# First MoE's first product as plain 512-column products beside the attention, instead of seven products for eight

## The chip, the cores and the metric

The kernel runs on one core of one Trainium2 chip. The metric is the device time of one execution in microseconds (us); less is better. Of several executions the median is given. A profile is one execution taken by the hardware profiler; its span runs from the first to the last instruction.

## The reference

Three stages follow each other: causal attention with a decay, then two MoE layers (each one a dense pair of products, without routing). Cut to what is computed:

```python
# q, k, v: (4, 8, 576, 64), f: (4, 8, 576)
cum = cumsum(log(clip(f, 1e-4, 1)))                      # per batch and head
scores = q @ k.T / sqrt(64) + cum[:, None] - cum[None, :]
attn = softmax(where(causal, scores, -1e9)) @ v
x = attn, heads side by side                             # (2304, 512)
h = x @ w_in;  g = h * clip(h + 3, 0, 6) / 6;  x = g @ w_out      # first MoE, w_in (512, 2048)
h = x @ w_in2; g = softplus(h);                out = g @ w_out2   # second MoE
```

The weight matrices arrive as 64-bit floats, and the kernel turns their words into 32-bit floats itself.

## The kernel before, in words

**The work.** The attention goes by 16 pairs of heads (4 batches of 4 pairs). For a pair: q and k are loaded in runs of 32 elements and transposed by VectorE (`qk_job`, L563); the scores are products of 64 rows (`s_job`, L609), VectorE takes the row minimum with the decay added (L631) and ScalarE the exponential (L640); TensorE transposes the result (`t_job`, L703; copied out at L725), multiplies it with v (`pv_job`, L750), and VectorE scales by the inverse of the row sums, which went through DRAM to be spread over the partitions (`inv_job`, L674, L758). The pair's x goes to DRAM (L763). The decays come from DRAM too (L568), for the first pair from TensorE (`first_decays`, L583).

**The four MoE products** are made seven for eight (the Strassen-Winograd scheme: seven products of sums of quarter matrices instead of eight of the quarters). Each product of 32-bit numbers is three matmuls of rounded parts: high x high, high x low, low x high. So every factor is split by ScalarE (high part, a copy with rounding) and VectorE or GpSimd (low part, a difference).

- First product of the first MoE: `step_a(0, t, p)`, four blocks t of 576 tokens (a batch each), eight pairs p of 128-column tiles of w_in. A step is 7 products x 2 x 3 = 42 matmuls of 288 columns (L1064). They are summed by ScalarE copies (L1080) and VectorE additions (L1083), then come Relu (L1108) and a min-and-multiply (L1109), and a store of g (L1116).
- Its x factors, `factors_x(0, t)`: loads from DRAM (L998), four differences (L1022) and seven splits (L1017, L1018). For t < 3 all blocks use the one buffer MX, and the differences lie in HY[0], the tile into which the products are summed; `freed(hkeys(0), fours)` and back order the two uses.
- Its weight factors, `weights(0, 0, p)`: two loads of 512 KB into two staging tiles (L858), conversion (L878, L880, L881), four sums (L925), splits into U[p] (L954, L957).
- Second product: `step_c`, blocks of 512 and 256 tokens, 42 or 21 matmuls of 256 columns a step (L1220), g loaded from DRAM and factored (`factors_g`, L1151, L1162, L1173, L1177); its weights are converted earlier and stored in DRAM (`convert`, L888), loaded again (L913), and factored by `weights(0, 1, p)`.
- The second MoE follows in the same way: `step_a(1, t, p)` (L1064), `step_b` (L1275).

**The order.** All operations are given to a planner (`Work.order`) with a cost, a due time `at` and what they read and write. It goes through them in its own model of time and writes one fixed order for each engine; transfers nearly all go through SP's queue in that order. On the chip an engine waits for whatever its next instruction needs. The due times come from the table `PLAN`: T0, D1, D2, D3 place the blocks of the first product beside the attention, b0 and the gaps place the ends of the batches, u0 to u3 and c1 to c3 the weights; capA and capH limit the PSUM banks that attention and first product hold (eight in all).

**The tiles.** In the attention's time the space on the right holds two more sets of score tiles (pc, pd) and a second xs. They are closed after pair 5 (NZ = 6) to make room for U[6] and U[7]; from pair 6 on there are two sets and one xs. After the attention `open_m2` opens XO, HY[1], XT, GR and two more staging tiles; the last x block of the first product goes to XO, and so waits for it.

Of the kernel before, what the change touches and what calls it, by code (L numbers as in the profile page):

```python
# [20 lines left out]
S_JOBS = [[[(4, 0, 288)], [(4, 288, 576)]], [[(3, 0, 448)]], [[(2, 0, 320)], [(1, 0, 192), (0, 0, 64)]]]  # L21
# [30 lines left out]
    NZ=6,  # L52
    pc=4087.38,
    pp=2327.32,
    pv=84.33,
    bend=[1.23, 1.22, 0.82, 0.85],
    b0=45.58,
    T0=63.44,
    D1=71.18,
    D2=126.72,  # L60
    D3=92.29,
    gap=35.47,
    gap2=34.18,
    gap3=57.23,
    cA=2.46,
    SA=5.95,
    SC=5.87,
    SB=2.2,
    iva=10.96,
    nwarm=18,  # L70
    sp=-2.13,
    evb=-2.3,
    u0=-9.63,
    u1=6.1,
    u2=12.94,
    u3=4.01,
    fx=-4.74,
    ul=20.0,
    c1=18.83,
    c2=53.66,  # L80
    c3=7.91,
    cvw=16.39,
    ldw=121.83,
    xa=36.77,
    xs=3.98,
    ga=3.94,
    tsp=-32.98,
    xat=0.0,
    xl=6.7,
    rel=96.88,  # L90
    wfrom=22.68,
    lv0=9.67,
    lq1=14.03,
    decst=4.47,
    capH=3,
    capA=8,
    eps=0,
    slp=45.39,
    slv=33.59,
    lat=1.39,  # L100
# [200 lines left out]
def attention_two_moe_kernel(  # L301
# [24 lines left out]
    NA, NG = S, 2 * P  # L326
    CB = [(0, TB), (TB, NG)] + [(TB + NG + i * TB, TB) for i in range((NT - TB - NG) // TB)]
# [18 lines left out]
    g1_dram = [dp.tile([NF, P, S], F32, name=f"g1_dram{b}") for b in range(B)]  # L346
# [33 lines left out]

    T0 = K["T0"]

    BLK = [T0, T0 + K["D1"], T0 + K["D1"] + K["D2"], T0 + K["D1"] + K["D2"] + K["D3"]]
    MC = BLK[3] + K["SA"] * NPR
    M2_0 = MC + K["SC"] * NPR * NT / TB
    MB = M2_0 + K["SA"] * NPR * (NT // NA)

    def a_at(m, t, p, x=0.0):

        if m:  # L390
            return M2_0 + K["SA"] * (t * NPR + p + x)
        if t == 3:
            return BLK[3] + K["SA"] * (p + x)
        return BLK[t] + (BLK[t + 1] - BLK[t]) * ((p + x) / NPR) ** (K["cA"] if t == 0 else 1.0)
# [21 lines left out]

    IV = ap.tile([P, P], F32, name="bar")
# [7 lines left out]
    MX = mp.tile([P, 7 * XW], F32R, name="MX")  # L425
# [11 lines left out]

    NZ = K["NZ"]
    FW = NPR - 2
    T = {}  # L440
    side = ctx.enter_context(ExitStack())
# [22 lines left out]
    def open_early():  # L464
        a = side.enter_context(tc.tile_pool(name="apw", bufs=1, side="right"))
        T["xs"].append(a.tile([P, S], F32, name="xs2"))
        T["P"] = [PS, PS2]
        for z in "cd":
            t = a.tile([P, sum(PW)], F32, name="p" + z)
            T["P"].append([t[:, sum(PW[:i]):sum(PW[:i + 1])] for i in range(len(PW))])  # L470

    def set_of(pn, i):

        return (2 * pn + i) % 4 if pn < NZ else i

    U = []

    def open_late_w():
        side.close()
        a = ctx.enter_context(tc.tile_pool(name="lw", bufs=1, side="right"))  # L480
        for p in range(FW, NPR):
            U.append(a.tile([P, UW], F32R, name=f"U{p}"))

    st = [mp.tile([P, NC * P, 2], U32, name=f"st{i}") for i in range(2)]
    for p in range(FW):
        U.append(wp.tile([P, UW], F32R, name=f"U{p}"))

    op(("sp", 1.0, open_early), w=["early"], at=-9)
    openers = {"w": op(("sp", 1.0, open_late_w), w=["latew"], name="latew")}
# [4 lines left out]
    def fill_by(name, n, tiles, value, w, at=0.0, r=("early",), one=False):  # L494
        ways = [("pool", 0.9 * n + 60, lambda: nc.gpsimd.memset(tiles(), value)), ("dve", 1.04 * n + 8, lambda: nc.vector.memset(tiles(), value))]
        op(ways[:1] if one else ways, w=w, r=r, at=at, name=name)
# [4 lines left out]
    for i in range(2):  # L501
        fill_by("fv", P, lambda i=i: T["vr"][i][KCUT[-1][1]:, 4].rearrange("p h d -> p (h d)"), 0.0, [("vz", i)], one=True)
# [796 lines left out]
    for d in last_att:  # L1299
        for m in d.early:  # L1300
            openers[m].deps[d] = 1
# [111 lines left out]
```

## Time and profile before

| what | us |
|---|---|
| median of 3 runs | 994.32 (993.56 to 995.84) |
| profiled execution | 999.6 |
| its span | 997.8 |

In the profile's rows, L12 is line 12 of the kernel before. PE is TensorE's matmuls, PEld its weight loads, DVE VectorE, ACT ScalarE, POOL GpSimd, SP the engine that issues the transfers (SPq: its queue's instructions). A matmul's busy time is longer than its share of a steady run, since matmuls overlap; pace is therefore read from a stretch's length over its count. PEclk is the granted TensorE clock as a share of 2.4 GHz. `<-` in square brackets names what ended an idle time.

### The profile page before, as it was taken

What the parts mean: (1) busy time and instruction counts of PE and PEld (TensorE: products, weight loads), DVE (VectorE), ACT (ScalarE), POOL (GpSimd) and SP (SyncE); (2) the same over time, 40 slices, a digit from 0 to 9 for tenths busy, and PEclk for the clock granted to TensorE, in tenths of its full rate; (3) what the DMA queues carried; (4) which work ended last, traced back from release to release, by engine and by line L of the source; (5) the groups of instructions that cost most, each with busy time, mean ns of one, the idle gap of its engine ahead of it and who ended that gap; (6) DMA issues with size and microseconds to landing.
All of it is one profiled execution on the core that took longest, in us unless ns stands there. A gap on an engine that the chain in (4) does not pass through costs nothing.

```text
span 997.8 us, 19909 instructions
## 1 busy us (share of the span) xinstructions
PE 936.3 (94%) x7156; PEld 869.1 (87%) x7156; DVE 770.2 (77%) x1671; ACT 598.9 (60%) x1202; POOL 120.1 (12%) x250
## 2 busy tenths in 40 slices
PE   9888698988999898989999999999999989999997
PEld 5665587866896787989999999999999989999997
DVE  4676787967676767999879789988564877888885
ACT  3877777886777755864345355777566753333342
POOL 2232111220112002200010110300010100010000
PEclk6999899997999899998999999999999999999999
DMA  6778948799978686764553454699823643435342
GB/s 92 176 171 208 216 138 232 206 231 234 261 255 263 208 298 233 243 191 148 163 160 106 149 156 131 211 336 367 292 98 127 207 143 108 128 125 165 115 129 79
DMA packets 210467, 187.07 MB, mean 187 GB/s; under 512 B 108800, under 2 KB 161152, under 8 KB 210368
## 3 DMA queue, kind: packets, MB, share of 16 engines
q1 hardware_dynamic: 207744, 185.43, 62.4%
q8 instruction: 56, 0.92, 0.4%
q10 hardware_dynamic: 2624, 0.37, 0.3%
q14 instruction: 43, 0.35, 0.1%
HBM read 121.12 MB, written 64.63 MB: 186 GB/s over the span
## 4 chain that ended last, share of the span: by engine, by line
PE 66%; DVE 13%; DMA 10%; ACT 4%; issue 3%; SPq 2%; POOL 0%; ACTq 0%; DVEq 0%; POOLq 0%
PE bank L1064 31%; PE bank L1275 18%; PE bank L1220 10%; DVE MX L1177 2%; PE bank L609 2%; DMA st<-in_moe_w_in_dram 2%; DVE U L957 2%; PE bank L750 2%; PE bank L703 2%; SPq L527 1%; DMA st<-in_moe_w_out_dram 1%; DMA kr<-in_k_dram 1%; DVE st L925 1%; DVE HY L1162 1%; DMA ivb<-inv_dram 1%
## 5 line engine op out<-in xcount | busy, mean ns | idle before, releaser
L1064 PE MATMUL bank<-MX,U 128*128 128x288 f32 x1680 | 248.1, 304 | 17.1 <-ACT HY L1080 9.1
L1064 PEld LDWEIGHTS bank<-MX,U 128*128 128x128 f32 x1680 | 232.3, 192 | 27.2 <-ACT HY L1080 14.4
L1275 PE MATMUL bank<-U,XO 128*128 128x256 f32 x1512 | 181.4, 282 | 2.8 <-ACT XO L1173 2.0
L1275 PEld LDWEIGHTS bank<-U,XO 128*128 128x128 f32 x1512 | 180.7, 190 | 3.4 <-ACT XO L1173 2.2
L1220 PE MATMUL bank<-MX,U 128*128 128x256 f32 x1344 | 162.4, 282 | 5.0 <-DVE MX L1177 3.9
L1220 PEld LDWEIGHTS bank<-MX,U 128*128 128x128 f32 x1344 | 160.1, 190 | 6.6 <-DVE MX L1177 4.8
L1080 ACT ACTIVATE HY<-bank 128x288 f32<-128x288 f32 x256 | 101.2, 406 | 63.1 <-PE bank L1064 48.4
L1064 PE MATMUL bank<-XO,U 128*128 128x288 f32 x1008 | 137.6, 297 | 1.3 <-DVE HY L1083 1.1
L1064 PEld LDWEIGHTS bank<-XO,U 128*128 128x128 f32 x1008 | 135.2, 188 | 2.2 <-DVE HY L1083 1.6
L1083 DVE TENSOR_TENSOR HY<-HY,bank 128x288 f32<-128x288 f32 x192 | 84.8, 449 | 57.6 <-PE bank L1064 53.7
L624 POOL TENSOR_SCALAR_AFFINE_SELECT w<-w 128x128 f32<-128x128 f32 (+1 forms) x160 | 57.6, 368 | 240.9 <-DVE stats L631 173.8
L957 DVE TENSOR_TENSOR U<-st,U 128x768 fp32r<-128x768 f32 (+1 forms) x63 | 70.9, 1133 | 7.1 <-ACT U L954 6.9
L609 PE MATMUL bank<-KT,QT 64*128 64x288 f32 (+4 forms) x384 | 67.8, 446 | 8.7 <-ACT pt L725 6.6
L954 ACT ACTIVATE U<-st 128x1024 fp32r<-128x1024 f32 (+1 forms) x64 | 59.9, 949 | 12.1 <-DVE st L925 8.2
L725 ACT ACTIVATE pt<-bank 128x448 f32<-128x448 f32 (+2 forms) x127 | 57.6, 499 | 11.2 <-PE bank L703 10.0
L1108 ACT ACTIVATE HY<-HY,half 128x576 f32<-128x576 f32 x64 | 49.3, 774 | 21.5 <-DVE HY L1083 19.5
L609 PEld LDWEIGHTS bank<-KT,QT 64*128 64x128 f32 x384 | 39.0, 200 | 25.2 <-ACT pt L725 10.0
L1109 DVE SCALAR_TENSOR_TENSOR HY<-HY 128x576 f32<-128x576 f32 x64 | 49.8, 780 | 12.8 <-ACT HY L1108 12.6
L750 PEld LDWEIGHTS bank<-pt,vr 128*64 128x64 f32 x512 | 35.1, 142 | 23.6 <-DVE stats L631 5.5
L881 DVE SCALAR_TENSOR_TENSOR st<-st 128x512 uint32<-128x512 uint32 x64 | 44.3, 692 | 14.3 <-ACT st L878 10.6
L1173 ACT ACTIVATE MX<-GR 128x768 fp32r<-128x768 f32 x36 | 30.4, 844 | 40.6 <-PE bank L1220 33.6
L750 PE MATMUL bank<-pt,vr 128*64 128x256 f32 (+3 forms) x512 | 52.7, 352 | 1.3 <-DVE stats L631 0.9
(145 smaller groups left out, 1276.2 us busy)
## 6 DMA issues: line engine op xcount, KB each, us to landing
GR<-g_dram SPq DMA_DIRECT2D x52, 512.0 KB
g_dram<-HY SPq DMA_DIRECT2D x64, 288.0 KB
g_dram<-HY SPq DMA_DIRECT2D x32, 576.0 KB
st<-in_moe_w_in_dram SPq DMA_DIRECT2D x32, 512.0 KB
st<-in_moe_w_out_dram SPq DMA_DIRECT2D x32, 512.0 KB
wf_dram<-st SPq DMA_DIRECT2D x48, 256.0 KB
st<-wf_dram SPq DMA_DIRECT2D x48, 256.0 KB
w<-dec_dram SPq DMA_DIRECT2D x30, 288.0 KB
```

The source lines that it names most:

```text
L609: nc.tensor.matmul(bank[bks[h, y].i][:, o:o + c - a], T["Q"][z][h * D:h * D + D, q0:q0 + P], T["K"][z][h * D:h * D + D, a:c], start=lead, ...
L624: nc.gpsimd.affine_select(out=blk, in_=blk, compare_op=ALU.is_ge, fill=-1e9 / scale, base=0, pattern=[[-1, r]], channel_multiplier=1)
L725: e.activation(out=place(i, j, a, c), in_=src(), func=ACTF.Copy)
L750: nc.tensor.matmul(acc[i * D:i * D + D, s + k0 - a:c - a], T["vr"][z][:, j, i], place(i, j, s, c - k0), start=(n < 2), stop=(n >= len(todo ...
L954: op(("act", act(n * h, False), lambda src=src, to=to: nc.scalar.activation(out=to(0), in_=src(), func=ACTF.Copy)), r=rd, w=w, at=at, name ...
L957: e.tensor_tensor(to(1), src(), to(0).bitcast(F32), op=ALU.subtract)
L1064: nc.tensor.matmul(bank[bks[b].i][:, 0:HA], wa[u][:, c], xa[v][:, c], start=(nm in ("P1", "P2", "P5") and c == 0 and y == 0), stop=(c == 1 ...
L1080: op(("act", act(HA, True) + 30, lambda: nc.scalar.activation(out=to(q), in_=bp(), func=ACTF.Copy)), r=new, banks=[ba], w=[("H", i, q)], a ...
L1083: op(("dve", dve(HA), lambda: nc.vector.tensor_tensor(to(q), to(q), bp(), op=ALU.add)), r=new, banks=[ba], w=[("H", i, q)], at=at, name="a ...
L1109: op2(("dve", dve(n), lambda h=h: nc.vector.scalar_tensor_tensor(out=h(1), in0=h(1), scalar=1.0, in1=h(0), op0=ALU.min, op1=ALU.mult)), r= ...
L1220: nc.tensor.matmul(bank[bks[b].i][:, o * 256:(o + 1) * 256], *ops, start=(p == 0 and o == 0 and y == 0), stop=(p == NPR - 1 and y == 2), s ...
L1275: nc.tensor.matmul(bank[bks[b].i][:, o * 256:(o + 1) * 256], ga[u], wa[v], start=(p == 0 and o == 0 and y == 0), stop=(p == NPR - 1 and y ...
```

## The change

**The first product is plain.** Tokens go in blocks of 512 (four, and one of 256) and tiles `ft` of 128 columns of w_in, 16 of them. A step has 4 x 3 matmuls of 512 (or 256) columns into one bank, and no sums; Relu and the min-and-multiply read the bank:

```diff
+    GB = [(i * TB, min(TB, NT - i * TB)) for i in range(-(-NT // TB))]
...
+    def step_g(t, ft):
...
+        bk = Bank(att_banks, "h")
+        for c in range(NC):
+            def go(c=c):
...
+                for y, (w, x) in enumerate(((wh, xh), (wh, xl), (wl, xh))):
+                    nc.tensor.matmul(bank[bk.i][:, 0:n], w, x, start=(c == 0 and y == 0), stop=(c == NC - 1 and y == 2))
...
+        g = HY[0][:, i * TB:i * TB + n]
...
+        ev = at - K["evb"]
+        op(("act", act(n, True, 1) + 10, lambda: nc.scalar.activation(out=g, in_=bank[bk.i][:, 0:n], func=ACTF.Relu, scale=1.0 / 6.0, bias=half)), r=["half"], banks=[bk], w=[("g", i)], at=ev, name="relu")
+        op(("dve", dve(n), lambda: nc.vector.scalar_tensor_tensor(out=g, in0=g, scalar=1.0, in1=bank[bk.i][:, 0:n], op0=ALU.min, op1=ALU.mult)), banks=[bk], w=[("g", i)], at=ev, name="g")
+        dma(lambda: nc.sync.dma_start(out=g1_dram[ft, :, a0:a0 + n], in_=g), 4 * P * n, r=[("g", i)], w=[("gd", 0, t, ft)], at=at - 1, name="storeg")
```

`i` goes round four output buffers in HY[0]. g lies in one DRAM tensor over all tokens, so that the second product's loads of g are no longer cut at batch ends.

**Weights and x are only split.** `weights_g(ft)` loads and converts one tile and makes its high and low part. `load_g(t)` loads x by the four 128-row parts and splits each in place; block t lies in half t % 2 of MX. Block 0 is split from the attention's own tile:

```diff
+        if b == 0:
+            xh, xl = (XG(0)[z][:, hp] for z in range(2))
+            op(("act", act(TB, False), lambda: nc.scalar.activation(out=xh, in_=X()[:, 0:TB], func=ACTF.Copy)), r=xk, w=[("X", 0, hp)], at=at - K["xat"], name="xh")
+            op2(either(TB, lambda e: e.tensor_tensor(xl, X()[:, 0:TB], xh.bitcast(F32), op=ALU.subtract)), r=xk, w=[("X", 0, hp)], at=at - K["xat"], name="xl")
```

**Tiles.** The first product's weight parts W1 lie in the tiles U[3] to U[7]: ft 0 and 1 in U[3], seven parts each in the others. U[0] is free from the start, U[1] and U[2] are opened after the attention. Blocks 0 to 2 go beside the attention; the last two go together, tile by tile, and each unit of the second product's weights is made when the parts in its tile are used up:

```diff
+    for t in (LG, LG + 1):
+        load_g(t, BLK[3] - K["xa"] + 0.5 * (t - LG))
+    made = 3
+    for ft in range(NF):
+        for t in (LG, LG + 1):
+            step_g(t, ft)
+        while made < NPR and all(k[1] <= ft for k in on_tile[made]):
+            freed(on_tile[made], [("unit", made, 0), ("unit", made, 1)])
+            weights(0, 1, made, c_at(0, made) - K["u1"], made % 2 * 2, False)
+            made += 1
```

Unit 0 is made before, units 1 and 2 after `open_m2`.

**Attention.** `early`, `latew` and NZ go; all 16 pairs have four score sets and two xs. The scores are five jobs of at most one bank a head, and the first pair's heads go together too:

```diff
-S_JOBS = [[[(4, 0, 288)], [(4, 288, 576)]], [[(3, 0, 448)]], [[(2, 0, 320)], [(1, 0, 192), (0, 0, 64)]]]
+S_JOBS = [[[(4, 0, 288)]], [[(4, 288, 576)]], [[(3, 0, 448)]], [[(2, 0, 320)]], [[(1, 0, 192), (0, 0, 64)]]]
...
-        heads = (0, 1) if pn else (i,)
+        heads = (0, 1)
```

The first pair's decay matmuls use all 128 rows, for which GpSimd fills the other 96 rows of their tile with zeros:

```diff
-                    nc.tensor.matmul(bank[bk.i][:, 0:HA], ident[:BH, h:h + 1].to_broadcast([BH, P]), cum()[:, a:a + HA])
+                    nc.tensor.matmul(bank[bk.i][:, 0:HA], ident[:, h:h + 1].to_broadcast([P, P]), cum(P)[:, a:a + HA])
```

**The rest.** In the second product the g factors lie in XO and in the second MoE x starts in MX (before: the other way round), and the output tiles change places with HY. `PLAN` has new numbers throughout; among them capH 3 to 5, capA 8 to 7, and `pv`, the delay that `either` puts on VectorE before it prefers GpSimd, 84 to 0.

## Rows read from the trace of the kernel before

**Rows 1.** Busy us (instructions) of each engine, by stretch; then PEclk, DMA share, GB/s.
```profile
0.00:94.00 94.00, 79.71 (x484) 56.47 (x484) 58.56 (x204) 62.53 (x180) 27.17 (x100) 0.86 0.75 159
94.00:121.00 27.00, 17.60 (x143) 13.87 (x139) 18.82 (x49) 18.55 (x44) 5.36 (x13) 0.93 0.94 210
121.00:205.00 84.00, 80.62 (x604) 69.78 (x604) 72.43 (x189) 66.27 (x160) 12.84 (x29) 0.98 0.71 197
205.00:239.00 34.00, 27.49 (x200) 18.25 (x198) 24.87 (x77) 25.56 (x70) 5.87 (x21) 0.88 0.87 224
239.00:333.00 94.00, 87.13 (x639) 74.97 (x640) 66.37 (x192) 69.92 (x179) 14.45 (x38) 0.94 0.85 254
333.00:391.00 58.00, 51.41 (x362) 47.76 (x362) 41.13 (x78) 33.55 (x67) 5.00 (x3) 0.97 0.75 258
391.00:452.00 61.00, 56.57 (x421) 55.53 (x420) 57.28 (x99) 43.62 (x78) 7.71 (x8) 0.98 0.67 218
```

**Rows 2.** TensorE in two even stretches: 288 columns (L1064), then 256 (L1220).
```profile
640.00:700.00 60.00, 60.00 (x449) 1.00 0.92 326
510.00:545.00 35.00, 35.00 (x303) 1.00 0.45 125
```

**Rows 3.** Chain of waits: start, us, engine, line; scores L609, transposes L703, values L750.
```profile
129.89 1.17 PE bank L609 x8
132.85 0.95 PE bank L609 x4
138.00 1.89 PE bank L750 x20
141.68 1.23 PE bank L609 x12
...
286.58 1.13 PE bank L750 x12
...
296.86 1.64 PE bank L703 x15
```

**Rows 4.** First product's matmuls (L1064), two stretches; the second product's (L1220), the latter.
```profile
121.00:205.00 84.00, 52.50 (x335) 0.98 0.71 197
391.00:452.00 61.00, 48.24 (x359) 0.98 0.67 218
...
391.00:452.00 61.00, 9.14 (x62) 0.98 0.67 218
```

**Rows 5.** Timelines of VectorE, SP's queue and TensorE: x of batch 0's fourth pair.
```profile
84.77 0.81 DVE L758 TENSOR_TENSOR xs<-bank,ivb 128x256 f32<-128x256 f32 x2
...
93.87 0.54 SPq L763 DMA_DIRECT2D x_dram<-xs  x1
106.45 1.10 SPq L998 DMA_DIRECT2D MX<-x_dram  x2
...
120.98 8.91 PE L1064 MATMUL bank<-MX,U 128*128 128x288 f32 x53 [2.10 <-DVE MX L1018]
```

**Rows 6.** Groups by line, 0 to 452 us: busy us, mean ns, idle before.
```profile
L1109 DVE SCALAR_TENSOR_TENSOR HY<-HY 128x576 f32<-128x576 f32 x64 | 49.8, 780 | 12.8 <-ACT HY L1108 12.6
L1083 DVE TENSOR_TENSOR HY<-HY,bank 128x288 f32<-128x288 f32 x96 | 42.7, 448 | 24.2 <-PE bank L1064 21.0 <-ACT HY L1080 1.8 <-ACT HY L1108 0.9
L957 DVE TENSOR_TENSOR U<-st,U 128x1024 fp32r<-128x1024 f32 (+1 forms) x29 | 31.4, 1095 | 0.0
L1018 DVE TENSOR_TENSOR MX<-HY,MX 128x576 fp32r<-128x576 f32 x12 | 8.9, 758 | 0.0
L1080 ACT ACTIVATE HY<-bank 128x288 f32<-128x288 f32 x128 | 50.5, 406 | 33.7 <-PE bank L1064 19.1 <-DVE HY L1109 14.3
L1108 ACT ACTIVATE HY<-HY,half 128x576 f32<-128x576 f32 x64 | 49.3, 774 | 21.5 <-DVE HY L1083 19.5 <-DVE U L957 0.6 <-DVE st L880 0.6
```

**Rows 7.** As rows 1, at the first pair's start.
```profile
15.00:20.00 5.00, 5.00 (x11) 2.53 (x12) 1.21 (x6) 1.63 (x4) 0.59 (x2) 0.50 0.45 79
```

**Rows 8.** Chain of waits: a load of the second product's weights.
```profile
445.45 2.66 DMA st<-wf_dram
```

More of the change, by code (lines that the diff above doesn't have):

```diff
@@ L51 @@
 PLAN = dict(
[L52 to L69, printed above, removed]
-    nwarm=18,
[L71 to L77, printed above, removed]
-    ul=20.0,
[L79 to L96, printed above, removed]
+    pc=78.633,
+    pp=1626.916,
+    pv=0,
+    bend=[1.119, 1.0, 1.0, 0.9],
+    b0=47.858,
+    T0=59.215,
+    D1=96.614,
+    D2=81.65,
+    D3=81.326,
+    D4=70.932,
+    gap=16.562,
+    gap2=18.0,
+    gap3=23.337,
+    cA=1.111,
+    SA=5.521,
+    SC=4.964,
+    SB=2.386,
+    iva=9.172,
+    nwarm=18,
+    sp=0.871,
+    evb=-0.48,
+    u0=6.93,
+    u1=47.121,
+    u2=5.548,
+    u3=2.95,
+    fx=-1.856,
+    ul=20.0,
+    c1=9.498,
+    c2=13.359,
+    c3=23.635,
+    cvw=0,
+    ldw=48.152,
+    xa=-3.322,
+    xs=-1.161,
+    ga=4.306,
+    tsp=-10.459,
+    xat=36.251,
+    xl=1.582,
+    rel=32.858,
+    wfrom=7.28,
+    lv0=7.543,
+    lq1=4.785,
+    decst=1.735,
+    capH=5,
+    capA=7,
     eps=0,
-    slp=45.39,
-    slv=33.59,
-    lat=1.39,
+    slp=0,
+    slv=0,
+    lat=1.649,
 )
@@ L345, in attention_two_moe_kernel @@
     dec_dram = dp.tile([B * H, S], F32, name="dec_dram")
-    g1_dram = [dp.tile([NF, P, S], F32, name=f"g1_dram{b}") for b in range(B)]
+    g1_dram = dp.tile([NF, P, NT], F32, name="g1_dram")
     g_dram = dp.tile([NF, P, NT], F32, name="g_dram")
@@ L415, in attention_two_moe_kernel, with XG @@
     ident = mp.tile([P, P], F32, name="ident")
+    def XG(t):
+        z = t % 2 * 2 * NC * TB
+        return [MX[:, z + y * NC * TB:][:, 0:NC * TB].rearrange("p (c n) -> p c n", c=NC) for y in range(2)]
     IV = ap.tile([P, P], F32, name="bar")
@@ L734, in pv_job @@
         z = pn % 2
[L735 to L736 removed]
+        y = z
+        wk.mark = ()
         bk = Bank(att_banks, "a")
@@ L811, in attention @@
                         t_job(prev[0] * HP + prev[1], prev[2], idx, at - K["tsp"])
-                    elif what == "s" and cur and not (i and n):
-                        s_job(n, i, idx, at - (K["sp"] if n < NZ else 0))
+                    elif what == "s" and cur and not i:
+                        s_job(n, i, idx, at - K["sp"])
                     elif what == "v" and prev and prev[2]:
@@ new lines, in load_g, with xt @@
+    def load_g(t, at):
+        a0, n = GB[t]
+        done = 0
+        while done < n:
+            b, o = divmod(a0 + done, S)
+            cnt = min(n - done, S - o)
+            for c in range(NC):
+                dma(lambda b=b, o=o, cnt=cnt, done=done, c=c: nc.sync.dma_start(out=XG(t)[1][:, c, done:done + cnt].bitcast(F32), in_=x_dram[b][c, :, o:o + cnt]),
+                    4 * P * cnt, r=[("xd", b, c)], w=[("X", t % 2, c)], at=at + 0.1 * c, name="loadx")
+            done += cnt
+        for c in range(NC):
+            def xt(c=c):
+                return [x[:, c, 0:n] for x in XG(t)]
+            op(("act", act(n, False), lambda xt=xt: nc.scalar.activation(out=xt()[0], in_=xt()[1].bitcast(F32), func=ACTF.Copy)), w=[("X", t % 2, c)], at=at + 0.1 * c, name="xh")
+            op2(either(n, lambda e, xt=xt: e.tensor_tensor(xt()[1], xt()[1].bitcast(F32), xt()[0].bitcast(F32), op=ALU.subtract)), w=[("X", t % 2, c)], at=at + 0.1 * c, name="xl")
@@ L1037, in open_m2 @@
             st.append(sb.tile([P, NC * P, 2], U32, name=f"st{2 + i}"))
+        for p in (1, 2):
+            U[p] = sb.tile([P, UW], F32R, name=f"U{p}")
     def hy(i):
@@ L1047, in step_a @@
     def step_a(m, t, p):
-        first = m == 0 and t < B - 1
-        z, i = xbuf(m, t), 0 if first else (t * NPR + p) % 2
-        bks = [Bank(list(range(8)), "h" if first else "s") for _ in range(3)]
+        z, i = xbuf(m, t), (t * NPR + p) % 2
+        bks = [Bank(list(range(8)), "s") for _ in range(3)]
         factor = {nm: (a, f) for nm, _, a, f in SEVEN}
```

213 lines of the change are left out of this document (99 added, 114 removed).

## The prediction

> **What bounds the kernel now.** I read the stretches of the span first [rows 1]: one row each, with the busy time and instruction count of every engine. Look at TensorE's count against the length. Two even stretches give its steady pace [rows 2]: 60 / 449 = 133.6 ns for a 288-column product, 35 / 303 = 115.5 ns for a 256-column one. The chain of waits [rows 3] holds the attention's pieces at their pace: scores 1.17 + 0.95 + 1.23, two times 1.64 for 30 transposes, 1.89 + 1.13 for the values: 9.65 us for 86 instructions, 0.112 each. So the work of a stretch can be computed, and what is left over I call lost.
>
> The first MoE's first product is 4 blocks x 8 pairs x 42 = 1344 matmuls (179.6 us). From 94 to 452 us TensorE did 2369 instructions: these, 62 of the second product (7.2 us), and 963 of the attention (107.9). That is 294.7 us of work in 358: **63.3 us lost, 17.7%**. From 0 to 94 it did 440 attention instructions (49.3 us; 44 warm-up ones aside), and that stretch is paced by transfers. After 452 come 1512, 1344 and 1512 matmuls at nearly these paces; the change leaves those counts alone.
>
> Where are the 63 us? With the product's own counts [rows 4], 121 to 205 holds 335 x 0.1336 + 269 x 0.112 = 74.9 us of work and loses 9.1 (10.8%); 391 to 452 loses 5.8 (9.5%). The seams are worse: 94 to 121 loses 10.9 and 205 to 239 loses 11.6, with two and no matmuls of the MoE. The other 152 us lose 25.9. The first seam can be followed [rows 5]: the last two x parts of batch 0's fourth pair are in SBUF at 85.6, their store is issued at 93.9, the last loads at 106.5, and the first run of products starts at 121.0, held by VectorE's factors. From 391 to 452 VectorE is busy 57.3 of 61 us: evacuation and weight factors crowd each other there.
>
> **The change, part by part.** *Product.* It takes out 1344 matmuls and puts in 16 x 12 x 4 = 768 of 512 columns and 192 of 256. No row shows 512 columns. Below: a 256-column one plus 256 columns at the full 2.4 GHz, 115.5 + 106.7 = 222 ns. Above: the 288-column pace in proportion, 237.5. I take 232, because the two rows lie 18 ns apart for 32 columns, steeper than either end assumes. So 178.2 + 22.2 = 200.4 us, **20.8 us more TensorE work** (13.1 to 25.0).
>
> The Trainium skill, TensorE: Matmul & The Clock Gate, section Back-to-back issue gap, gives columns / 2.4 GHz + 2.5 ns for a warm matmul, 215.8 ns at 512. By it the new product would take 12.5 us less than I count. The trace doesn't agree at 256 columns, where the rule says 109.2 and the row 115.5.
>
> *Evacuation.* Before, VectorE spends 49.8 + 42.7 us and ScalarE 50.5 + 49.3 on it [rows 6]. After, each block and tile takes one Relu out of PSUM and one combined min-and-multiply. For 512 columns I estimate 0.71 us on VectorE (0.448 for 288, at the slope to 0.780 for 576) and 0.69 on ScalarE (between 0.406 and 0.774): 52 and 50 us in all, so 40 and 49 less. Both now read the bank, which stays taken a little longer; that is covered while other banks are open.
>
> *Factors.* Eleven VectorE operations per x block at 0.758 (44, 33.4 us) become 20 splits of up to 512 columns (about 12). Sixteen weight splits of 1.095 become sixteen of about 0.67, and the sums before them go. Together VectorE sheds at least 67 of its 339.5 us before 452, and falls from 75% to about 63%. That alone gains nothing: it counts where VectorE ended a wait.
>
> *Buffers.* x has two buffers and no longer borrows the evacuation tile, so block t+1 can be split while block t multiplies; block 0 skips DRAM. This aims at the seams. What is late next is the attention itself, since block 0 needs its fourth pair at 85.6. Filling 86 to 94 at half use: 4 us.
>
> *SP's queue.* x loads go from 16 to 28 and stores of g from 64 to 80; the loads of g fall from 56 to 36, most of them later. 28 issues of about 0.5 us [rows 5] are 14 us of queue, ahead of q, k and weight loads that wait behind them. Bounds 0 to 14; I take 2, because the queue issues while TensorE works on earlier blocks. A store that waits for VectorE holds the next q and k loads; four rotating output buffers make that rarer.
>
> *Attention.* All pairs get four score sets and two x tiles: a wait removed, at no cost. Scores go in five jobs on fewer banks; the same matmuls. The first pair waits for both heads' q and k: 0 to 2 us, hidden behind the decay matmuls. Those now use 128 rows; TensorE runs there at a granted 0.50, its 1.2 GHz level [rows 7]. If it rises earlier, the first pair gains up to 5 us; two GpSimd fills ahead of it cost up to 1.3 by my estimate. I take a gain of 1.
>
> *Factors of the second product.* Units 0 to 2 have tiles of their own, 3 to 7 take tiles that hold first-product weights and come free as these finish. Per unit: two loads, four sums, two ScalarE and two VectorE splits, as before. Unit 7 is made only behind the last product, and 7 steps of 42 x 0.1155 = 4.9 us of second product cover it, but beside VectorE's factors of g. Nothing as long as VectorE keeps up; else the wait for one weight load (2.66 us) [rows 8] per late unit. I take 3, ends 0 and 6. Where `either` now sends more to GpSimd, nothing, off the path.
>
> *Last two blocks.* They need batch 3's x through DRAM. From load issue to the first run of products took 121.0 - 106.5 = 14.5 us for block 0 [rows 5]; block 2's 192 matmuls, 44.5 us, cover that. After 452 only buffers change places: 0, between -3 and +3.
>
> **The sum.** Work after 94: 294.7 - 7.2 + 20.8 - 4 = 304.3 us. What share is lost? 121 to 205 (10.8%) and 391 to 452 (9.5%) are seamless stretches, but with VectorE 86% and 94% busy. At 63% I take 8%, ends 5 and 11. That gives 304.3 / 0.92 = 330.8, and the second product starts at 94 + 330.8 + 3 + 2 - 1 = 428.8, against 452 - 7.2 = 444.8: 16.0 us earlier. The profiled execution took 999.6 (span 997.8, 1.8 around it), so 983.6. The median of the runs is 994.32, 5.3 below that execution; carried over, **978 us**. With 5 and 11% it is 968 and 989, and with the matmul bounds this forecast's own range is 962 to 993.
>
> **Rivals.** *Slower: the loss stays.* TensorE gets 20.8 us more work, and the share lost remains 17.7%, because it belongs to SP's queue and the transfers, not to VectorE or buffers: 304.3 / 0.823 = 369.7, the second product starts at 467.7, 22.9 later, **1017 us**. It decides above a loss of 12.3% (304.3 / 346.8). For it: DMA shares of 0.94, 0.87 and 0.85 in the stretches that lose most [rows 1], and more issues on SP. Against it: TensorE's first run waited on VectorE [rows 5].
>
> *Faster: the wide matmul pays its fixed part less often.* At 222 ns and a 5% loss, (304.3 - 7.7) / 0.95 = 312.2, the start is at 410.2, 34.6 earlier: **960 us**. For it: VectorE relieved. Against: the two paces of [rows 2], in proportion to columns or steeper. By the Trainium skill's rule quoted above alone, with 8% lost, it would be 964; the trace speaks against that rule at 256 columns.
>
> *No change: the last x path stands bare.* If the static order spends block 2 before the attention ends, those 14.5 us are added once: **992 us**. Against it: the order is planned with that load's cost in it.
>
> **Chances.** Forecast 0.52, faster rival 0.18, slower rival 0.22, bare path 0.08. A measurement of this kernel can tell about 0.2%, 2 us, from no change. So faster 0.70, same 0.08, slower 0.22. The range reaches down to 953, under the faster rival by its matmul bound, and up to 1010, which takes in half of the slower rival: the loss need not stay whole.
>
> **What would show it.** Right: 768 + 192 matmuls at about 232 ns; the first of them near 86 to 95 us; no stretch of 20 us between 95 and 430 without MoE products; VectorE near 63% before the second product; that product's first run near 429; about 553 us from there to the span's end, as before (997.8 - 444.8). Wrong: the first product after 110; a loss above 12%, with TensorE released by DMA or SP's queue; a pace above 240 ns; idle of several us at the start of the second product for U; a second half that differs by over 3 us.

## The result, and the profile after

The changed kernel took 957.52 us (median of 4 runs, 955.56 to 962.84), the kernel before, beside it, 995.08 (993.56 to 1001.07): a ratio of 0.962, 95% interval 0.9564 to 0.9676. That is 37.6 us faster; 978 was forecast. The profiled execution took 956.72 us (span 954.9) against 999.6 (span 997.8) before. The mean granted clock over the span is 0.994.

The stretches after, as in [rows 1]; the last one ends where the second product starts, so that its numbers hold one kind of work:

```profile
0.00:94.00 94.00, 82.14 (x558) 58.71 (x560) 65.10 (x216) 69.57 (x195) 31.52 (x103) 0.98 0.89 194
94.00:121.00 27.00, 26.47 (x168) 18.08 (x165) 17.85 (x52) 17.38 (x44) 3.70 (x12) 1.00 0.91 239
121.00:205.00 84.00, 79.78 (x470) 57.20 (x469) 51.73 (x156) 56.11 (x147) 13.35 (x38) 0.96 0.86 229
205.00:239.00 34.00, 32.82 (x208) 23.37 (x206) 17.64 (x48) 18.92 (x48) 3.10 (x11) 1.00 0.80 217
239.00:333.00 94.00, 93.87 (x594) 68.44 (x595) 54.16 (x165) 61.64 (x156) 11.54 (x37) 1.00 0.82 247
333.00:406.00 73.00, 73.00 (x412) 63.34 (x412) 52.54 (x104) 35.98 (x61) 5.90 (x3) 1.00 0.80 265
```

TensorE is busy 305.9 of the 312 us from 94 to 406; before it was 320.8 of 358 from 94 to 452. Its clock column is 1.00 in four rows of six; in [rows 1] no row reaches that. The DMA share is no lower than before (0.80 to 0.91), and none of TensorE's waits in this stretch is put down to a load.

The chain of waits after (start, us, engine, line, count); L1008 is the first product, L1256 the second:

```profile
156.25 4.90 PE bank L1008 x21
...
314.93 3.50 PE bank L1008 x15
...
332.80 72.99 PE bank L1008 x408
405.80 4.57 PE bank L1256 x39
```

Two things stand here. The pace of a 512-column matmul is 4.90 / 21 = 233 ns, and 3.50 / 15 gives the same. The long run holds all that is left of the 192 narrow ones; if it holds all of them, it gives (72.99 - 192 x 0.1155) / 216 = 235 ns. And the second product starts at 405.8 us, where the forecast had 428.8.

The first product's groups up to 406 us, against [rows 6] (busy us, mean ns, then the idle time before and what ended it; the mean mixes 512 and 256 columns):

```profile
L1008 PE MATMUL bank<-MX,U 128*128 128x512 f32 (+1 forms) x960 | 235.7, 387 | 3.7 <-DVE stats L638 2.4 <-DVE HY L1014 0.7 <-DVE MX L773 0.4
...
L1013 ACT ACTIVATE HY<-bank,half 128x512 f32<-128x512 f32 x80 | 50.0, 641 | 49.1 <-PE bank L1008 44.2 <-DMA g_dram<-HY 4.5
```

The Relu, which now reads the bank first, waits for the product (44.2 us) and hardly for anything else. In [rows 6] the operation that reads the banks first, ScalarE's copy L1080, waited 14.3 us for the step before to leave its tile. TensorE's own waits say the same. First the kernel before, waits of the weight load and of the matmuls from 94 to 452 (us, times, longest):

```profile
PEld bank L1064 <- ACT HY L1080: 14.4, 17, 3.3
...
PE bank L1064 <- ACT HY L1080: 9.1, 10, 3.1
```

Then the changed kernel, 94 to 406; no evacuation is among its longest waits, and "issue" is time in which nothing was waited for:

```profile
PEld bank L1008 <- issue: 7.8, 18, 0.7
...
PEld bank L1008 <- DVE stats L638: 2.8, 2, 2.5
```

**Where the time came from.** Work up to the second product is 1403 attention instructions (440 + 963 before; 157.1 us) and the first product: 179.6 us before, 200.4 by the forecast's 232 ns. Against the starts at 444.8 (452 less the 62 matmuls of the second product done by then) and 405.8, the time lost falls from 108.0 to 48.3 us. The stretches allow an estimate of two parts of this loss. TensorE's idle time (length less busy) goes from 14.3 + 37.2 = 51.5 us to 11.9 + 6.1 = 18.0. The clock's part, (1 - granted clock) x length, goes from 13.2 + 17.9 = 31 us to 1.9 + 3.1 = 5. So of some 60 us recovered, about 33 were idle time and, by this estimate, 26 a clock that is now at its full level; 21 were spent again on the extra matmul work. Low clock during idle time is in both parts, so the split is rough. After the second product starts, 549.1 us remain, where 553.0 did before.

Where the idle time was matters for what follows. From 94 to 333 us, the kernel before and the changed one (columns as above):

```profile
94.00:333.00 239.00, 212.84 (x1583) 176.86 (x1580) 182.49 (x503) 180.30 (x450) 38.52 (x100) 0.94 0.81 225
```

```profile
94.00:333.00 239.00, 232.94 (x1435) 167.10 (x1432) 141.38 (x421) 154.04 (x392) 31.68 (x98) 0.99 0.84 235
```

Of the 37.2 idle us of the kernel before, 26.2 lie here; the changed kernel has 6.1. The 9.1 us in which TensorE's matmuls waited for the copies L1080 are a quarter of the 37.2.

### The profile page after: what moved, and what is told of

Its sections match the earlier page's. It is cut to its first block, busy times and chain, and to the rows that moved or that the text cites. A ratio compares the mean times of both kernels' runs of the same rounds, so it can differ in the third digit from the quotient of the medians.

```text
span 954.9 us, 18734 instructions
## 1 busy us (share of the span) xinstructions
PE 929.1 (97%) x6772; PEld 827.2 (87%) x6772; DVE 698.9 (73%) x1548; ACT 541.5 (57%) x1082; POOL 100.8 (11%) x238
## 4 chain that ended last, share of the span: by engine, by line
PE 73%; DVE 11%; DMA 9%; ACT 3%; issue 2%; SPq 1%; POOL 0%; ACTq 0%; DVEq 0%; POOLq 0%
PE bank L1008 19%; PE bank L1311 19%; PE bank L1112 14%; PE bank L1256 10%; PE bank L710 4%; PE bank L757 3%; PE bank L616 3%; DVE XO L1213 3%; DMA st<-in_moe_w_out_dram 2%; DVE U L964 2%; DMA GR<-g_dram 2%; DMA st<-in_moe_w_in_dram 2%; DMA kr<-in_k_dram 1%; DVE HY L1229 1%; ACT pt L732 1%
## 5 line engine op out<-in xcount | busy, mean ns | idle before, releaser
L1008 PE MATMUL bank<-MX,U 128*128 128x512 f32 (+1 forms) x960 | 235.7, 387 | 3.7 <-DVE stats L638 2.4
L1008 PEld LDWEIGHTS bank<-MX,U 128*128 128x128 f32 x960 | 158.8, 190 | 39.9 <-issue 9.0
L1311 PE MATMUL bank<-U,MX 128*128 128x256 f32 x1512 | 179.9, 281 | 0.0
L1311 PEld LDWEIGHTS bank<-U,MX 128*128 128x128 f32 x1512 | 179.6, 189 | 0.0
L1256 PE MATMUL bank<-XO,U 128*128 128x256 f32 x1344 | 159.2, 280 | 0.5 <-DVE XO L1213 0.5
L1256 PEld LDWEIGHTS bank<-XO,U 128*128 128x128 f32 x1344 | 158.4, 189 | 0.9 <-DVE XO L1213 0.7
L1112 PE MATMUL bank<-MX,U 128*128 128x288 f32 x672 | 92.4, 297 | 1.3 <-ACT HY L1128 0.9
L1112 PEld LDWEIGHTS bank<-MX,U 128*128 128x128 f32 x672 | 90.3, 188 | 2.7 <-ACT HY L1128 1.4
L1112 PEld LDWEIGHTS bank<-XO,U 128*128 128x128 f32 x672 | 90.4, 188 | 0.7 <-DVE HY L1131 0.5
L1013 ACT ACTIVATE HY<-bank,half 128x512 f32<-128x512 f32 x80 | 50.0, 641 | 49.1 <-PE bank L1008 44.2
L732 ACT ACTIVATE pt<-bank 128x384 f32<-128x384 f32 (+2 forms) x127 | 58.8, 496 | 29.5 <-PE bank L710 26.8
L1014 DVE SCALAR_TENSOR_TENSOR HY<-HY,bank 128x512 f32<-128x512 f32 x80 | 49.4, 631 | 35.0 <-ACT HY L1013 34.1
L1128 ACT ACTIVATE HY<-bank 128x288 f32<-128x288 f32 x128 | 50.4, 406 | 27.2 <-PE bank L1112 26.8
L964 DVE TENSOR_TENSOR U<-st,U 128x1024 fp32r<-128x1024 f32 (+1 forms) x48 | 52.8, 1113 | 5.0 <-ACT U L961 4.9
L1153 ACT ACTIVATE HY<-HY 128x576 f32<-128x576 f32 x64 | 43.7, 684 | 20.5 <-DVE HY L1131 17.0
L616 PEld LDWEIGHTS bank<-KT,QT 64*128 64x128 f32 x384 | 32.1, 187 | 26.5 <-issue 8.0
```

The costliest lines, as they stand in the source:

```text
L616: nc.tensor.matmul(bank[bks[h, y].i][:, o:o + c - a], T["Q"][z][h * D:h * D + D, q0:q0 + P], T["K"][z][h * D:h * D + D, a:c], start=lead, ...
L732: e.activation(out=place(i, j, a, c), in_=src(), func=ACTF.Copy)
L964: e.tensor_tensor(to(1), src(), to(0).bitcast(F32), op=ALU.subtract)
L1008: nc.tensor.matmul(bank[bk.i][:, 0:n], w, x, start=(c == 0 and y == 0), stop=(c == NC - 1 and y == 2))
L1013: op(("act", act(n, True, 1) + 10, lambda: nc.scalar.activation(out=g, in_=bank[bk.i][:, 0:n], func=ACTF.Relu, scale=1.0 / 6.0, bias=half) ...
L1014: op(("dve", dve(n), lambda: nc.vector.scalar_tensor_tensor(out=g, in0=g, scalar=1.0, in1=bank[bk.i][:, 0:n], op0=ALU.min, op1=ALU.mult)), ...
```

## The experiments

All times are medians; a ratio is to the kernel before, run beside it. To read them, it helps to know what another instruction order by itself does, so that comes first.

**The order alone.** One constant of the planner's costs:

```
-    lat=1.649,
+    lat=1.7,
```

> The changed kernel with one number of the planner's model moved (lat 1.649 to 1.7), so that it writes another order of the same operations. It has no theory: it says how far a new order alone moves the time, against which every experiment that makes the planner write anew must be read. If the gain comes from the operations and buffers, it stays within 5 us of 957.5; if it comes from one lucky order, it is 10 us or more above.

Measured: 949.62 us, ratio 0.9521 (0.9487 to 0.9555). The same operations in another order (a few on another engine) are 8 us faster than the changed kernel, more than the 5 us expected. TensorE's row is nearly full (columns as above):

```profile
94.00:400.00 306.00, 303.36 (x1847) 226.96 (x1846) 191.26 (x519) 188.88 (x450) 34.78 (x103) 1.00 0.86 246
```

This version beats both kernels. It also sets a measure for what follows: where an edit lets the planner write a new order, some 8 us either way can be the order's doing, and only a larger difference, or one with its wait in the trace, is read as a cause. The 8 us are a single draw, so the spread may be wider.

**The tables of due times, exchanged.** The whole of `PLAN`: due times, delays, and the bank limits capH and capA (3 and 8 in the kernel before, 5 and 7 in the changed one). The changed kernel with the table of the kernel before (a few of the diff's lines), then the kernel before with the new one:

```
-    T0=59.215,
-    D1=96.614,
...
+    T0=63.44,
+    D1=71.18,
...
```

> The changed kernel's operations with the table of due times and costs of the kernel before (D4 kept, which that table lacks). Rival under test: the gain comes from the new table, not from the operations; then this lies at 985 or above. Theory (operations and buffers): most of the gain stays, 960 to 975, since another order alone moved the time by 8 us.

> The kernel before with the table of due times and costs of the changed kernel (NZ kept, D4 unused). If the table is what the gain comes from, this is well below 994: 975 or less. If operations and buffers are, it lies within 10 us of 994 or above it.

Measured: 962.39 us, ratio 0.9649 (0.9618 to 0.9681), and 1017.42, ratio 1.0201 (1.0162 to 1.024). The new constants do not carry the gain; the kernel before is 20 us slower with them. The first of the two also had three banks for the product, as many as the kernel before, and its 5 us are within the order's spread.

**VectorE's relief, taken back.** A second VectorE operation on every g tile, behind the release of the bank; it changes no value:

```
         op(("dve", dve(n), ...), banks=[bk], w=[("g", i)], at=ev, name="g")
+        op(("dve", dve(n), lambda: ...(out=g, in0=g, scalar=1.0, in1=g, op0=ALU.mult, op1=ALU.max)), w=[("g", i)], ...)
```

> The changed kernel with one more VectorE operation of 512 columns per block and tile, on the output tile, which changes no value: about 53 us of VectorE work are given back. Theory (VectorE's relief is why the share lost fell from 17.7% to 6.5%): 10 us or more slower, 968 or above. Rival (buffers and order did it, VectorE has room): within 5 us of 957.5, 953 to 962.

Measured: 957.14 us, ratio 0.9598 (0.9567 to 0.9628): no cost. From 94 to 406 us, this kernel and then the changed one (columns as above; VectorE is the third pair):

```profile
94.00:406.00 312.00, 303.69 (x1836) 228.99 (x1833) 230.47 (x584) 189.67 (x458) 61.32 (x120) 0.99 0.83 241
```

```profile
94.00:406.00 312.00, 305.94 (x1846) 230.43 (x1843) 193.92 (x523) 190.03 (x452) 37.58 (x101) 0.99 0.83 242
```

The added operations take 53.1 us. The plan hands some other work to GpSimd for it, so VectorE's own busy time over the span rises by 40.4 us (739.3 against 698.9). In this stretch it is busy 74% instead of 62%, and TensorE's busy time falls by 2.2 us. VectorE's load, the forecast's reason for a smaller loss, is not why the loss is small now.

**An earlier start.** In the changed kernel the first product's first matmul runs at 33.4 us, long before batch 0 is whole. Three edits: block 0 waits for all its x; block 0 goes through DRAM as the others; no product before batch 1's first x has been stored.

```
-            ... r=[("W1", ft, 0), ("W1", ft, 1), ("X", t % 2, c)], ...
+            ... r=[("W1", ft, 0), ("W1", ft, 1)] + [("X", t % 2, x) for x in ([c] if t else range(NC))], ...
```

> In the changed kernel the first product's matmuls of block 0 wait for all four parts of x, as the prediction assumed, instead of part by part. Theory (the product fills gaps of the attention before 94 us, which I priced at 4 us instead of 16): some 10 to 14 us slower, 968 to 972, and no matmul of the product before 70 us. Rival (the gain comes from the seams and from VectorE's relief after 94 us): the work only moves, under 4 us, 958 to 961.

```
-        if b == 0:
+        if False:
...
-        if t:
-            load_g(t, BLK[t] - K["xa"])
+        load_g(t, BLK[t] - K["xa"])
```

> In the changed kernel block 0 also takes its x through DRAM, like the other blocks, still part by part. Theory (the early fill is what I mis-sized): the parts come about 10 us later each, so part of the fill goes; 3 to 8 us slower, 961 to 966. Rival (seams): the first product starts late as it did before the change, but work is there later; under 3 us.

```
-            ... ("X", t % 2, c)], w=[bk], ...
+            ... ("X", t % 2, c)] + [("xd", 1, 0)] * (t == 0), w=[bk], ...
```

> The changed kernel, in which block 0's products wait until x of batch 1's first pair is in DRAM, which puts their start near 110 us, about where it was before the change. Theory of products as filler: some 16 us of products leave the first 94 us, and what they leave idle is lost unless later waits take them up; the kernel that waited for all four parts lost nothing, so the point where it costs is tested here: 5 to 12 us slower, 963 to 970. Rival (start is of no account, only the later seams are): within 4 us of 957.5.

Measured: 955.28 us, ratio 0.9576 (0.9549 to 0.9604); 963.29, 0.9651 (0.9618 to 0.9684); 957.28, 0.9609 (0.958 to 0.9637). All within the order's 8 us. The second lies where its theory had it; in the other two the theory fell. In the last one no product at all runs before 94 us, and its first two stretches are emptier, but the later ones are full:

```profile
0.00:94.00 94.00, 74.89 (x535) 52.28 (x535) 65.97 (x225) 69.59 (x199) 28.65 (x105) 0.95 0.91 191
```

```profile
94.00:121.00 27.00, 24.59 (x144) 18.15 (x141) 18.78 (x54) 19.71 (x51) 4.15 (x13) 1.00 1.03 246
...
239.00:333.00 94.00, 94.00 (x589) 68.54 (x586) 54.40 (x164) 61.57 (x156) 11.14 (x36) 1.00 0.80 241
333.00:406.00 73.00, 73.00 (x425) 62.57 (x423) 53.86 (x105) 37.65 (x62) 6.81 (x4) 1.00 0.79 263
```

It has done 535 - 44 = 491 attention instructions by 94 us, the changed kernel 558 - 69 - 44 = 445. What is not filled with the product is filled with attention, which then no longer has to be waited for. The early start, which looks like the gain in the profile, is not by itself the cause of it.

**Buffers of x and depth of the attention.** One x buffer for all blocks (written with the last two blocks still side by side, so both of them multiply block 4's x: the time is read, not the output); then the last two blocks one after the other, with two buffers and with one; then two score sets and one x tile from the seventh pair on, as before.

```
-        z = t % 2 * 2 * NC * TB
+        z = 0
...
-    ... w=[("X", t % 2, c)], ...
+    ... w=[("X", 0, c)], ...
```

> The changed kernel with one x buffer for all blocks, as before the change: block t+1 can't be split while block t multiplies. Theory (the seams went because of the second buffer): idle at three block ends comes back, 12 us or more slower than 957.5, so 970 or above, and stretches of 10 us and more without the product's matmuls. Rival (VectorE's relief and the smaller evacuation did it): under 6 us.

```
-    for ft in range(NF):
-        for t in (LG, LG + 1):
-            step_g(t, ft)
+    for t, ft in [(t, ft) for t in (LG, LG + 1) for ft in range(NF)]:
+        ...
+        step_g(t, ft)
```

> The changed kernel, but the last two blocks go one after the other (all 16 tiles of the 512-token block, then all 16 of the 256-token block) instead of tile by tile together, so that the tiles of the second product's weights come free during the 256-token block only. It is the base for the next kernel. Expected: 957.5 to 962, since units 3 to 7 are made within 22 us of products and into the second product's first block. If making the units as tiles come free early matters much: 967 or above.

> The kernel just above with one x buffer for all blocks instead of two. Theory (the share lost fell because products of some block are always ready to fill the attention's waits, which the second buffer provides): 12 to 20 us slower than the kernel above, with idle TensorE at each block's end, most of it at the two ends behind the attention. Rival (the order of the last two blocks explains the 974.9 of the kernel with one buffer): within 6 us of the kernel above.

```
-        return (2 * pn + i) % 4
+        return (2 * pn + i) % 4 if pn < 6 else i
...
-        y = z
+        y = z if pn < 6 else 0
```

> The changed kernel with two score sets and one xs from pair 6 on, as before the change. Theory (products fill the waits, so the attention's own depth matters little): within 8 us of 957.5, the spread that another order alone gives. Rival (deeper attention is a main part of the gain): 968 or above, with the product waiting for x of batches 2 and 3.

Measured: 974.86 us, ratio 0.9776 (0.9738 to 0.9814); in turn 956.08, 0.9601 (0.9563 to 0.9639); in turn with one buffer 962.63, 0.9663 (0.9629 to 0.9697); two sets 958.24, 0.9631 (0.9592 to 0.9669). From 333 to 406 us, for one buffer, in turn, and in turn with one buffer (the second product starts at 427.8, 404.7 and 416.6 us):

```profile
333.00:406.00 73.00, 56.09 (x316) 47.31 (x316) 50.28 (x98) 32.69 (x54) 0.89 (x1) 0.88 0.79 260
```

```profile
333.00:406.00 73.00, 73.00 (x413) 63.14 (x412) 50.02 (x96) 34.40 (x56) 7.50 (x5) 1.00 0.78 258
```

```profile
333.00:406.00 73.00, 66.34 (x321) 53.53 (x320) 47.19 (x87) 33.06 (x51) 5.65 (x5) 0.95 0.78 258
```

TensorE's wait for the split of x in these 73 us, for one buffer and for one buffer in turn (us, times, longest):

```profile
PE bank L1008 <- ACT MX L991: 15.3, 1, 15.3
```

```profile
PE bank L1008 <- ACT MX L991: 5.0, 2, 4.7
```

The second x buffer is worth 6.5 us where the blocks go in turn, between what theory and rival expected. That is no more than another order can make, but its wait is in the trace: 5.0 of the 73.0 - 66.3 = 6.7 idle us. It is worth more where both last blocks need theirs at once: 15.3 us of waiting. For the score sets from the seventh pair on nothing can be told from the order's spread. Where TensorE stands idle here, the clock falls as well: 0.88 and 0.95 against 1.00.

**The clock at the start.** The decay matmuls with 32 rows again in the changed kernel, and with 128 rows in the kernel before (with the fills that this needs):

```
-   ident[:, h:h + 1].to_broadcast([P, P]), cum(P)[:, a:a + HA]
+   ident[:BH, h:h + 1].to_broadcast([BH, P]), cum()[:, a:a + HA]
```

> The changed kernel with the first pair's decay matmuls on 32 rows again, the order of every engine kept. Theory (the clock at the start is worth the 1 us I took): the granted clock is 0.5 from 10 to 30 us again, and the time rises by 0 to 2 us, since transfers pace that stretch. Rival (the first 30 us set when batch 0 ends, and so everything): 5 us or more slower.

> The kernel before with the first pair's decay matmuls on 128 rows and the fills for it. Theory (clock at the start): the granted clock from 10 to 30 us rises from about 0.5 to near 1, and the time falls by 2 to 8 us, 987 to 993, since 11 us of the first 94 went to the low clock. Rival (transfers pace that stretch): within 3 us of 996.

Measured: 960.19 us, ratio 0.963 (0.9588 to 0.9673), and 990.49, ratio 0.9943 (0.9917 to 0.997). The stretch of [rows 7], where the granted clock was 0.50, in the changed kernel, in it with 32 rows, and in the kernel before with 128:

```profile
15.00:20.00 5.00, 3.39 (x24) 2.40 (x24) 3.44 (x16) 5.00 (x20) 2.48 (x6) 1.00 0.97 262
```

```profile
15.00:20.00 5.00, 3.89 (x22) 2.45 (x21) 3.52 (x11) 2.89 (x8) 2.07 (x5) 0.73 0.84 223
```

```profile
15.00:20.00 5.00, 4.54 (x31) 3.61 (x31) 3.68 (x18) 4.64 (x16) 1.35 (x5) 1.00 0.67 154
```

With 128 rows the clock is at its 2.4 GHz level there, with 32 it is not. In the kernel before that is worth 0.6%, and it is not another order's doing: in both traces TensorE, VectorE and ScalarE run the same lines in the same order (GpSimd's differs by the fills). In the changed kernel, also in an unchanged order, it can't be told from nothing.

**The evacuation, undone.** Two output buffers instead of four, two banks in flight instead of five, and on every g tile one more VectorE and one more ScalarE operation, which change no value:

```
-    capH=5,
+    capH=2,
...
-        i = ngb[0] % 4
+        i = ngb[0] % 2
...
+        op(("dve", ...(out=g, in0=g, scalar=1.0, in1=g, op0=ALU.mult, op1=ALU.max)), w=[("g", i)], ...)
+        op(("act", ...activation(out=g, in_=g, func=ACTF.Copy)), w=[("g", i)], ...)
```

> The changed kernel with the product's evacuation made like that of before: two output buffers (1024 columns, where before one tile of 1152 was used), two banks in flight, and one more operation each on VectorE and ScalarE per block and tile (which change no value), some 50 us each. Theory A (evacuation held the products before: TensorE waited for ScalarE's copies, rows 6): 15 us or more slower, 973 or above, TensorE idle in front of the products. Theory B (only what fills the waits counts): 950 to 965.

Measured: 992.78 us, ratio 0.9944 (0.9921 to 0.9968). This is the large one: 0.0324 of 995, 32 us, about as much as the whole gain. But it is not the loss of the kernel before come back. From 94 to 333 us, where that kernel's TensorE was idle for 26.2 us:

```profile
94.00:333.00 239.00, 234.08 (x1433) 165.53 (x1430) 163.79 (x458) 172.06 (x428) 39.68 (x101) 0.99 0.84 235
```

It is idle for 4.9 us here, at a clock of 0.99: no worse than in the changed kernel. The new loss comes later. The second product starts at 435.3 us, some 30 later than in the changed kernel; the rest of the 38.1 us by which its profiled span is longer lies behind that start. The stretches from 333 us on, where the first product runs almost alone:

```profile
333.00:391.00 58.00, 49.60 (x247) 41.29 (x246) 46.59 (x89) 31.66 (x53) 5.74 (x5) 0.91 0.77 254
391.00:452.00 61.00, 48.95 (x274) 42.28 (x273) 41.38 (x74) 30.65 (x55) 3.04 (x4) 0.94 0.38 123
```

TensorE stands idle 20.5 of 119 us, at a clock of 0.91 and 0.94; in the kernel before it was 11.0 of the same 119. Its waits there, from 333 to 452 us (us, times, longest; L1258 is the second product, from 435 us on):

```profile
PE bank L1008 <- DVE HY L1014: 6.5, 7, 3.0
PE bank L1008 <- ACT MX L991: 6.1, 1, 6.1
PE bank L1258 <- DVE HY L1014: 4.7, 3, 2.3
```

11.2 us are waits for L1014, the min-and-multiply that leaves a bank free; 6.1 are a single wait for the split of x on ScalarE; why that came late was not followed.

And the Relu, which stands ahead of L1014, waits for the store of an output buffer and not for the product:

```profile
L1013 ACT ACTIVATE HY<-bank,half 128x512 f32<-128x512 f32 x79 | 49.5, 641 | 31.7 <-DMA g_dram<-HY 28.9 <-PE bank L1008 2.4 <-ACT pc L647 0.2
```

In the kernel before nothing of the kind is seen: [rows 6] names no store among the main waits of L1080, L1083, L1108 and L1109, and the copies waited for the step before instead. So the edit makes the evacuation shallow again, but another wait stands in it.

**Its parts.** The output buffers alone (the middle lines of that diff), and the two operations alone (its last lines):

> Two output buffers instead of four, five banks and the short chain kept. If the Relu's wait for the store of g makes the loss (buffers): 975 to 990, with ScalarE's Relu behind the store in the waits. If the number of banks in flight or the two more operations make it: 957 plus or minus 6.

> One more VectorE and one more ScalarE operation on each g tile behind the bank's release (about 50 us of each engine; no value changes), four buffers and five banks kept. If the busy time and the longer chain to the store make the loss: 975 to 990. If the depth of buffers and banks covers them: 957 plus or minus 6.

Measured: 971.09 us, ratio 0.9722 (0.9676 to 0.9769), and 962.73, ratio 0.9637 (0.9594 to 0.968). The product's and the Relu's groups up to 452 us, with two buffers and then with the two operations:

```profile
L1008 PE MATMUL bank<-MX,U 128*128 128x512 f32 (+1 forms) x960 | 235.8, 388 | 12.2 <-DVE HY L1014 9.3 <-DVE stats L638 1.8 <-DVE MX L773 0.6
...
L1013 ACT ACTIVATE HY<-bank,half 128x512 f32<-128x512 f32 x80 | 49.5, 639 | 46.9 <-DMA g_dram<-HY 36.7 <-PE bank L1008 6.1 <-DMA MX<-x_dram 2.1
```

```profile
L1008 PE MATMUL bank<-MX,U 128*128 128x512 f32 (+1 forms) x960 | 235.3, 387 | 7.1 <-DVE HY L1014 4.8 <-ACT pt L732 1.1 <-DVE MX L773 1.0
...
L1013 ACT ACTIVATE HY<-bank,half 128x512 f32<-128x512 f32 x80 | 49.8, 637 | 13.3 <-PE bank L1008 10.7 <-DMA g_dram<-HY 1.0 <-ACT HY L1016 0.7
```

The two operations take 53.3 us on VectorE and 45.8 on ScalarE, and they cost nothing that can be told from the order's spread, with four buffers and five banks beside them, though TensorE's wait for L1014 goes from 0.7 to 4.8 us. Two buffers put the store into the Relu's path (36.7 us of waiting, 4.5 with four), TensorE then waits 9.3 us for L1014, and it costs 10 us. That is less than the 975 expected of buffers as the whole loss, and more than the rival allowed. The remaining 20 of the 32, give or take what the order does, come only with two banks instead of five, alone or together with the other two parts; two banks alone were not tried. The kernel before had three, and the changed kernel ran with three at 962.39 us, so these 20 us are not shown to be a part of the old loss.

**Everything but the evacuation undone, and both.** The diffs of the last two blocks in turn, of one x buffer, of two score sets and of the late start, all in one kernel; then these with the diff of the evacuation and with 32 rows:

> The changed kernel with the last blocks in turn, one x buffer, two score sets from pair 6 on, and block 0 waiting for x of batch 1's first pair in DRAM, all together. Theory B (products must always be ready to fill the attention's waits; singly each part is made up by the others): 975 or above, well over the 962.6 of one buffer alone. Theory A (evacuation): 962 to 968.

> The two kernels just above in one, with the decay matmuls on 32 rows too. What remains of the change is the plain product itself with its 20.8 us of more matmul time and shorter factors. If these parts are the whole cause, the share lost is back near 17% and the time at 1000 to 1017; if what is left over (factor chains, order) carries a good part, 970 to 990.

Measured: 973.79 us, ratio 0.9764 (0.9702 to 0.9827), and 1001.82, ratio 1.0044 (1.0021 to 1.0068). The first lies between the two theories, the second where it was expected if these parts were the whole cause. Together the parts that cost little one by one cost 14 us, and with the evacuation 42: then the kernel is slower than before, with the wide product and its new plan kept. In this last kernel the second product starts at 446.8 us; against the work of 357.5 us it loses 89 us, where the kernel before lost 108. Those 19 us that remain are not assigned. And again the loss lies elsewhere. From 94 to 333 us, in this last kernel:

```profile
94.00:333.00 239.00, 226.79 (x1402) 167.33 (x1399) 160.57 (x450) 169.77 (x422) 37.43 (x97) 0.99 0.82 228
```

TensorE is idle 12.2 us there, the kernel before 26.2, and the clock is at 0.99 instead of 0.94. So some 14 us of idle time, and the clock that went with it, stay recovered with all these parts of the change undone. What no run undid are the wide product itself, the shorter factors of x and weights, the scores in five jobs and the new places of the tiles. The cause of these 14 us may lie in any of them; this rival is untested.

## Why the prediction was right or wrong

**Right.** The added work: 16 x 12 x 4 wide matmuls at 233 to 235 ns against 232, so 200.4 us of product stands to within 3. The rule quoted from the Trainium skill, TensorE: Matmul & The Clock Gate, section Back-to-back issue gap, gives 215.8 ns at 512 columns, for an isolated warm matmul; the trace does not agree, by 17 ns. The forecast's 12.5 us by that rule count the wide matmuls alone. VectorE came to 62% busy, where 63 was forecast. Of the two causes put into the faster rival, the cheaper matmul fell and the smaller loss came near: 6.6%, between its 5 and the forecast's 8. The loss did fall, and not for SP's queue: the product's waits name no load, though the DMA share stayed at 0.80 to 0.91. So the slower rival, a loss that belongs to transfers and remains at 17.7%, fell. The last x path was covered, as the forecast had it; with one x buffer, in turn, 5.0 us of it stood bare.

**Wrong: how much of the loss goes.** The forecast's span was 981.8 us and came out at 954.9, 26.9 less. By its own terms:

- "Filling 86 to 94 at half use: 4 us": 69 matmuls and 5 attention instructions more, 16.5 us. That is 12.5. In the kernel before, the first x store of batch 0 is issued at 55.5 us already; the forecast let the product wait for the last, with a start near 86 to 95 us; it was 33.4.
- The share lost after 94, taken at 8%: 405.8 - 94 = 311.8 us hold 291.1 us of work (699 x 0.232 + 192 x 0.1155 + 953 x 0.112), so 20.7 are lost, 6.6%, against 26.5 forecast. That is 5.8.
- The separate 3 + 2 - 1 us for late units, SP's queue and the clock: in the loss already, 4.0.
- From the second product's start to the end: 549.1 against 553, 3.9, which is over the 3 us that the forecast allowed for buffers changing places. Its cause was not followed. The rest is 0.7.

So the step that failed is the loss up to the second product: 71 us forecast (44.7 - 4 + 26.5 + 4), 48 measured, 108 before. Splitting it at 94 us was itself a mistake. The run without any product before 94 shows that what is not filled early is filled later, and the time stays. The sum has to be made over the whole of attention and first product.

**The reason given was wrong too.** The forecast tied the loss to VectorE (75% falling to 63% busy) and said of the rotating output buffers only that stores would hold the queue less. VectorE did fall, but giving it back operations of 53 us cost nothing. What the runs show in its place is that the small loss of the changed kernel needs depth: two output buffers instead of four cost 10 us, with two banks and a longer chain beside them 32, and x buffer, score sets, late start and blocks in turn together 14.

What made the loss of the kernel before is shown only in part. A step there could not begin to leave its banks until the step before had left its one tile, which [rows 6] shows as 14.3 us of L1080's waiting for L1109, with 14.4 us of TensorE's weight loads and 9.1 of its matmuls behind it. The forecast read these rows for their busy time and not as a chain of operations with one buffer. But 9.1 are a quarter of the 37.2 idle us, and no edit brought back the 26.2 between 94 and 333 us: undoing the evacuation gave 4.9 there, undoing everything that was undone 12.2. That part of the cause stays open.

**The clock at the start** was taken at 1 us with up to 5 possible; the kernel before gained 0.6% by it, about 6 us, which is the term's upper end. In the changed kernel its loss can't be told from nothing.

## What to carry to other kernels

Before a loss is put down to a busy engine, read what its operations waited for: an evacuation that waits for its own previous step or for a store lacks buffers. Here 53 us more work on VectorE were free, and two output buffers less were not. When a part of a change is undone, look whether the old loss comes back at its old place: one of the same size somewhere else, as here behind 333 us, does not show the cause. Sum what is lost over the whole region in which one kind of work can fill the gaps of another, not by stretches. And where the order is planned, plan it a few times: one constant gave 8 us here, more than most single edits.

## What the runs showed that was not expected

An idle TensorE was mostly paid for twice. With the x buffers, where it was busy 56.1 of 73 us the mean granted clock was 0.88, where 66.3 it was 0.95, where 73.0 it was 1.00; by the estimate above, some 26 of the 60 us recovered by the change are clock. It isn't in proportion: with the evacuation undone, 8.4 idle us of 58 went with 0.91 and 12.1 of 61 with 0.94. Nor does row count leave the clock alone: with 128 rows in the decay matmuls the granted clock between 15 and 20 us is 1.00, with 32 rows 0.50 to 0.73. And the wide matmul runs in proportion to its columns, 233 ns for 512 against 115.5 for 256 [rows 2]: no fixed part that could be saved shows in these two paces.
